# First attention of a pooled-attention and two-MLP kernel: how half of the heads is exponentiated, and where the first weight conversion is asked for

## The chip, the cores and the metric

The kernel runs on one core of one Trainium2 chip. The metric is device microseconds of one execution; of the kernel before three runs are shown, with a median of 1615.76 us (1615.23 to 1616.89). One further execution was profiled, and every row below comes from it.

## The reference

The inputs are `q`, `k`, `v` of shape 8 x 8 x 576 x 64 (batch, heads, positions, head width) in fp32. Keys and values are averaged over groups of 8 positions, which leaves 72 of each.

```python
scores = scale * np.matmul(q, k_p.transpose(0, 1, 3, 2))
scores = scores - np.max(scores, axis=-1, keepdims=True)
attn = np.exp(scores)
attn = attn / (np.sum(attn, axis=-1, keepdims=True) + 1e-09)
out = np.matmul(attn, v_p)
```

The result, 4608 tokens of width 512, goes through two MLPs (512 to 2048 to 512): the first with `h / (1 + exp(-h))`, the second with `h * clip(h + 3, 0, 6) / 6`. The MLP weights are fp64 and are turned into fp32 by the kernel itself from their two 32-bit words; that is the weight conversion spoken of below.

## The kernel before

The 4608 tokens are cut into 36 tiles of 128 rows, and four tiles make a group of 512 tokens, the unit of the MLPs. Matrix products are made of fp32 numbers split into a high and a low part.

Everything stands inside `with tc.manual_schedule()` (L686): the order in which the program asks for instructions is the order in which each engine has them, and no planner rearranges it. Loads go through the queue of SP.

**The first attention** (L709 to L774) makes the first four tiles, 0 to 3, before the first MLP's loop begins. Per tile:

- `scores` (L343) puts q times the pooled keys into two PSUM banks, one for each half of the heads (4 heads of 72 scores, 288 columns).
- `soft` (L742) turns scores into exponentials. For the first half, `below_max` (L366) takes the maxima on VectorE (L369) and subtracts them (L370), and `exps` (L376) is one exponential on ScalarE over 288 columns (L377). For the second half, `max_exps` (L379) takes the maxima on VectorE (L383), multiplies them by minus the scale (L384), and asks ScalarE for four exponentials of 72 columns with the maxima as bias, each of which also gives the sum of its row (L386).
- `turn` (L748) makes `norm` (L397) on VectorE: the sums of the first half (L401), two small instructions on the sums (L402, L405), and the product of all 576 columns with the inverse sums (L406). Then `probs_T` (L408) transposes the probabilities on TensorE (L417), behind some warming matmuls (L341), and ScalarE copies the result out (L418). For tile 3 the norm is asked for by itself (L764), ahead of its `turn`.
- `attend` (L753) is the product with the pooled values on TensorE (L457), and `split_x` splits it into a high part (ScalarE, L473) and a low part (VectorE, L474).

The order is soft 0, soft 1, turn 0, soft 2, turn 1, soft 3, attend 0, turn 2, norm 3, conversion, split 0, attend 1, turn 3, split 1, and so on. Tiles 0 and 1 share one buffer for the copied transposes, so the copies of tile 1 wait for attend 0.

**The weight conversion** is `conv_a` (L727), which takes the next piece from a list and calls `split_a` (L101). For the first piece that is a copy with a scale on ScalarE (L110), then a shift (L113), a shift-and-or (L116) and an and-or (L126) on VectorE, each of which needs the one before it. It issues no DMA and nothing on GpSimd. `conv_b` (L733) later makes the high part on ScalarE (L150) and the low part on GpSimd (L151). Four more pieces are converted at L775 to L778, and further ones in the loop.

**The loop** (L793) is over groups and over 16 slices of the hidden width: 12 matmuls of the first weight (L492), the activation (L506, L507), and the products with the second weight (L536 in the first group). Within the first group it also converts the remaining weights and makes the next attention tiles; their scores (L353) need the pooled keys of the second batch (L290 on VectorE).

Of the kernel before, what the change touches and what calls it, by code (L numbers as in the profile page):

```python
# [10 lines left out]
F32 = mybir.dt.float32  # L11
F32R = mybir.dt.float32r
U32 = mybir.dt.uint32
AF = mybir.ActivationFunctionType
ALU = mybir.AluOpType
AX = mybir.AxisListType
# [9 lines left out]
def kernel(  # L26
# [14 lines left out]
    nc = tc.nc  # L41
    B, NPAIR, P, S = k.shape
    H = 2 * NPAIR
# [13 lines left out]
    ESCALE = 1.0 / (POOL * math.sqrt(D))  # L57
# [5 lines left out]
    att = early.enter_context(tc.tile_pool(name="att", bufs=2))  # L63
# [37 lines left out]
    def split_a(layer, f, piece, mul=False):  # L101


        raw = w_raw.pop((layer, f, piece))
        hw = raw[:, :, 1]

        dst = raw[:, :, 1] if piece else None
        mag = att.tile([P, DM], F32, tag="wmag", name="wmag", bufs=4)
        bits = mag.bitcast(U32)
        nc.scalar.activation(mag, hw.bitcast(F32), AF.Copy, scale=2.0 ** -112)  # L110
        if mul:
            nc.scalar.activation(hw.bitcast(F32), hw.bitcast(F32), AF.Sign)
        nc.vector.tensor_scalar(  # L113
            out=bits, in0=bits, scalar1=3, scalar2=None, op0=ALU.logical_shift_left
        )
        nc.vector.scalar_tensor_tensor(  # L116
            out=bits, in0=raw[:, :, 0], scalar=29, in1=bits,
            op0=ALU.logical_shift_right, op1=ALU.bitwise_or,
        )
        if mul:  # L120
            nc.gpsimd.tensor_tensor(
                out=mag if dst is None else dst.bitcast(F32), in0=mag, in1=hw.bitcast(F32),
                op=ALU.mult,
            )
        else:
            nc.vector.scalar_tensor_tensor(  # L126
                out=bits if dst is None else dst, in0=hw, scalar=0x80000000, in1=bits,
                op0=ALU.bitwise_and, op1=ALU.bitwise_or,
            )
        if piece:  # L130
            w_whole[f] = dst.bitcast(F32)
        else:
            w_mag[layer, f, piece] = mag
# [179 lines left out]
    s_t = {}  # L313
    p_t = {}
# [47 lines left out]
    def new_pr(t, tag=None):  # L362
        pr = staging(tag, H * SP) if tag else prs[t % 2][:, :H * SP]
        p_t[t] = pr.rearrange("p (a h s) -> p a h s", a=2, s=SP)

    def below_max(t, a):  # L366
        sc = s_t[t][a]
        mx = att.tile([P, NPAIR, 1], F32, tag="mx", name="mx")
        nc.vector.tensor_reduce(out=mx, in_=sc, op=ALU.max, axis=AX.X)  # L369
        nc.vector.tensor_tensor(  # L370
            out=p_t[t][:, a], in0=sc, in1=mx.to_broadcast([P, NPAIR, SP]), op=ALU.subtract
        )
        if a == 1:
            s_t.pop(t)

    def exps(t, a):  # L376
        nc.scalar.activation(p_t[t][:, a], p_t[t][:, a], AF.Exp, scale=ESCALE)  # L377

    def max_exps(t, a):  # L379

        sc = s_t[t][a]
        mx = att.tile([P, NPAIR, 1], F32, tag="mx", name="mx")
        nc.vector.tensor_reduce(out=mx, in_=sc, op=ALU.max, axis=AX.X)  # L383
        nc.vector.tensor_scalar(out=mx, in0=mx, scalar1=-ESCALE, scalar2=None, op0=ALU.mult)  # L384
        for h in range(NPAIR):
            nc.scalar.activation(  # L386
                p_t[t][:, a, h], sc[:, h], AF.Exp, scale=ESCALE, bias=mx[:, h],
                accum_out=den_of(t)[:, a * NPAIR + h],
            )
        s_t.pop(t)  # L390

    def den_of(t):
        if t not in den_t:
            den_t[t] = att.tile([P, H, 1], F32, tag="den", name="den")
        return den_t[t]

    def norm(t, summed=0):  # L397
        pr = p_t[t].rearrange("p a h s -> p (a h) s")
        den = den_of(t)
        n = H - summed * NPAIR  # L400
        nc.vector.tensor_reduce(out=den[:, :n], in_=pr[:, :n], op=ALU.add, axis=AX.X)  # L401
        nc.vector.tensor_scalar(  # L402
            out=den, in0=den, scalar1=1e-9, scalar2=float(POOL), op0=ALU.add, op1=ALU.mult
        )
        nc.vector.reciprocal(out=den, in_=den)  # L405
        nc.vector.tensor_tensor(out=pr, in0=pr, in1=den.to_broadcast([P, H, SP]), op=ALU.mult)  # L406

    def probs_T(t, tags=A, tag=None, warm=0):  # L408
        pr = p_t.pop(t)
        pT = staging(tag, H * P)[:SP] if tag else att.tile([SP, H * P], F32, tag="pT", name="pT", bufs=1)  # L410
        pT = pT.rearrange("p (h t) -> p h t", t=P)
        for a in range(2):
            ps = bank(tags, a)
            if a == 0:
                keep_warm(ps, warm)
            for i in range(NPAIR):
                nc.tensor.transpose(ps[:SP, i * P:(i + 1) * P], pr[:, a, i, :], ident)  # L417
            nc.scalar.activation(  # L418
                pT[:, a * NPAIR:(a + 1) * NPAIR, :],
                ps[:SP].rearrange("p (h t) -> p h t", t=P),  # L420
                AF.Copy,
            )
        pT_t[t] = lambda h, o, n: pT[:, h, o:o + n]
# [26 lines left out]
    def weighted(t, tags=A):  # L450
        pT = pT_t.pop(t)
        ps = bank(tags, 0)
        for j in range(NPAIR):
            for o, n, b, _ in halves(t):
                for e in range(2):
                    h = 2 * j + e
                    nc.tensor.matmul(  # L457
                        ps[e * D:(e + 1) * D, j * P + o:j * P + o + n],
                        vp[b % 2][:, h * D:(h + 1) * D],
                        pT(h, o, n),  # L460
                        start=True,
                        stop=True,
                    )
        return ps

    def split_x(t, ps):
        g, i = divmod(t, TPG)
        if i == 0:
            new_x(g)
        xh, xl = xs[g]  # L470
        pv = ps.rearrange("p (j t) -> p j t", t=P)
        sl = slice(i * P, (i + 1) * P)
        nc.scalar.activation(xh[:, :, sl], pv, AF.Copy)  # L473
        nc.vector.tensor_tensor(  # L474
            out=xl[:, :, sl], in0=pv, in1=xh[:, :, sl].bitcast(F32), op=ALU.subtract
        )
# [209 lines left out]
    with tc.manual_schedule():  # L686
# [40 lines left out]
        def conv_a(n, mul):  # L727
            for i in range(n):
                if conv:
                    done.append(conv.pop(0))  # L730
                    split_a(*done[-1], mul=(i < mul))
# [10 lines left out]
        def soft(t):  # L742
            new_pr(t, f"o{4 + t}")
            below_max(t, 0)
            exps(t, 0)
            max_exps(t, 1)

        def turn(t):  # L748
            if t < 3:
                norm(t, 1)  # L750
            probs_T(t, banks[t], f"i{2 + t}" if t > 1 else None, WARM[t + 1] if t < 3 else 0)

        def attend(t):  # L753
            return weighted(t, [banks[t][0]])

        soft(0)
        soft(1)
        turn(0)
        soft(2)
        turn(1)  # L760
        soft(3)
        pv0 = attend(0)
        turn(2)
        norm(3, 1)  # L764
        conv_a(1, 0)
        split_x(0, pv0)
        pv1 = attend(1)
        turn(3)
# [23 lines left out]
        for layer in range(1):  # L792
            for g in range(NG):  # L793
# [4 lines left out]
                for f in range(NF):  # L798
                    n = (layer * NG + g) * NF + f
# [57 lines left out]
                    if 1 in now:  # L857
                        norm(t1)
# [163 lines left out]
```

## Time and profile before

| what | us |
|---|---|
| median of three runs | 1615.76 |
| the profiled execution's own time | 1616.97 |
| its span, first to last instruction | 1615.2 |
| PE busy | 1591.8 (99%) |
| DVE busy | 982.8 (61%) |
| ACT busy | 628.9 (39%) |
| POOL busy | 367.9 (23%) |

PE is TensorE, PEld its weight loads, DVE VectorE, ACT ScalarE, POOL GpSimd. The busy share is an average over the whole span; the stage of the change lies in the first 33 us. Times in rows count from the first instruction.

### The profile page before, as it was taken

How to read it: one execution, taken by the hardware profiler on the slowest of the kernel's cores; microseconds unless marked ns; L12 is line 12 of the kernel's file. 1: busy time of each engine (PE TensorE's matmuls, PEld its weight loads, DVE VectorE, ACT ScalarE, POOL GpSimd, SP SyncE). 2: the span in 40 equal slices, each digit the busy share in tenths (PEclk: the TensorE clock that was granted, in tenths of full speed). 3: DMA queues.
4: the chain of work that ended last, by engine and by line, in shares of the span. 5: the costliest groups of instructions: out<-in, count | busy, mean ns of one | idle time of the engine just before them, and what ended most of it. 6: DMA issues, size and time to landing. Idle time of an engine off the chain costs nothing.

```text
span 1615.2 us, 24007 instructions
## 1 busy us (share of the span) xinstructions
PE 1591.8 (99%) x9214; PEld 1386.5 (86%) x9214; DVE 982.8 (61%) x1592; ACT 628.9 (39%) x1094; POOL 367.9 (23%) x377
## 2 busy tenths in 40 slices
PE   7899999999999999999999999999999999999999
PEld 6455788888888888888888999999999999999998
DVE  7986666676776666665532555555646555656464
ACT  5343564333333333333332334343434343334333
POOL 4643353122312231311011021212121202020200
PEclk9999999999999999999999999999999999999999
DMA  9451245244443544343156634343434353534341
GB/s 282 148 193 41 97 153 163 91 162 149 142 137 121 162 155 131 122 141 126 68 195 208 223 106 159 114 157 105 157 105 157 105 164 98 170 98 163 105 131 53
DMA packets 101331, 224.27 MB, mean 139 GB/s; under 512 B 10464, under 2 KB 35936, under 8 KB 101216
## 3 DMA queue, kind: packets, MB, share of 16 engines
q1 hardware_dynamic: 101216, 222.73, 42.5%
q8 instruction: 73, 1.20, 0.3%
q14 instruction: 42, 0.34, 0.1%
HBM read 169.74 MB, written 52.95 MB: 138 GB/s over the span
## 4 chain that ended last, share of the span: by engine, by line
PE 92%; DVE 3%; DMA 3%; ACT 1%; issue 0%; SPq 0%
PE y L556 44%; PE hps L492 22%; PE p L631 17%; PE y L536 4%; PE aps L457 2%; PE aps L353 2%; ACT gh L654 1%; DVE gl L655 1%; DMA stage<-in_v_dram 1%; DVE t L647 1%; DMA stage<-in_q_dram 1%; DMA wraw<-in_moe_w_out_dram 1%; DVE u L903 0%; DMA wraw<-in_moe_w_in_dram 0%; DVE c L903 0%
## 5 line engine op out<-in xcount | busy, mean ns | idle before, releaser
L492 PE MATMUL hps<-x,whl 128*128 128x512 f32 x1728 | 403.4, 383 | 4.2 <-POOL whl L151 2.1
L492 PEld LDWEIGHTS hps<-x,whl 128*128 128x128 f32 x1728 | 326.1, 189 | 58.9 <-issue 8.0
L631 PEld LDWEIGHTS p<-xst,wst 128*128 128x128 f32 x3024 | 359.6, 192 | 7.6
L631 PE MATMUL p<-xst,wst 128*128 128x256 f32 x3024 | 360.3, 275 | 0.0
L556 PE MATMUL y<-whl,gh 128*128 128x512 f32 x1152 | 343.1, 379 | 0.2 <-ACT gh L654 0.2
L556 PE MATMUL y<-gh,whl 128*128 128x512 f32 x1024 | 310.0, 384 | 0.0
L556 PEld LDWEIGHTS y<-whl,gh 128*128 128x128 f32 x1152 | 207.3, 190 | 23.5 <-ACT gh L654 0.4
L619 POOL TENSOR_TENSOR xst<-xr,xst 128x512 fp32r<-128x512 f32 x63 | 83.4, 1325 | 614.4 <-ACT xst L618 574.7
L556 PE MATMUL y<-whl,gl 128*128 128x512 f32 x576 | 219.2, 381 | 0.6
L556 PEld LDWEIGHTS y<-gh,whl 128*128 128x128 f32 x1024 | 189.4, 189 | 29.4 <-issue 2.9
L556 PE MATMUL y<-gl,whl 128*128 128x512 f32 x512 | 194.6, 380 | 0.0
L655 DVE TENSOR_TENSOR gl<-t,gh 128x512 fp32r<-128x512 f32 x144 | 113.7, 790 | 131.1 <-ACT gh L654 131.1
L512 DVE SCALAR_TENSOR_TENSOR hps<-t,hps 128x512 f32<-128x512 f32 x128 | 88.2, 689 | 170.3 <-ACT t L511 169.7
L511 ACT ACTIVATE t<-hps 128x512 f32<-128x512 f32 x128 | 76.4, 597 | 263.8 <-PE hps L492 262.0
L654 ACT ACTIVATE gh<-t 128x512 fp32r<-128x512 f32 x144 | 119.6, 831 | 151.3 <-DVE t L647 151.3
L903 DVE TENSOR_TENSOR u<-u,p 128x512 f32<-128x512 f32 x180 | 120.1, 684 | 66.2 <-PE p L631 62.0
L193 POOL TENSOR_TENSOR hs<-hmag,hs 128x256 fp32r<-128x256 f32 x88 | 64.2, 734 | 411.2 <-ACT hs L192 367.3
L647 DVE SCALAR_TENSOR_TENSOR t<-t,u 128x512 f32<-128x512 f32 x108 | 90.8, 841 | 89.5 <-ACT t L646 89.5
L521 DVE TENSOR_TENSOR gl<-hps,gh 128x512 fp32r<-128x512 f32 x128 | 88.5, 691 | 85.1 <-ACT gh L520 85.1
L646 ACT ACTIVATE t<-u,three 128x512 f32<-128x512 f32 x108 | 77.4, 717 | 161.0 <-DVE u L903 161.0
L556 PEld LDWEIGHTS y<-whl,gl 128*128 128x128 f32 x576 | 108.8, 189 | 19.4 <-DVE gl L655 4.2
L520 ACT ACTIVATE gh<-hps 128x512 fp32r<-128x512 f32 x128 | 76.6, 598 | 123.8 <-DVE hps L512 123.8
(91 smaller groups left out, 1449.8 us busy)
## 6 DMA issues: line engine op xcount, KB each, us to landing
wst<-ws SPq DMA_DIRECT2D x156, 512.0 KB
ws<-hs SPq DMA_DIRECT2D x56, 256.0 KB
bl<-bT SPq DMA_DIRECT2D x28, 384.0 KB
x<-o SPq DMA_DIRECT2D x36, 256.0 KB
xr<-x SPq DMA_DIRECT2D x36, 256.0 KB
out_dram<-o SPq DMA_DIRECT2D x36, 256.0 KB
wraw<-in_moe_w_in_dram SPq DMA_DIRECT2D x16, 512.0 KB
wraw<-in_moe_w_out_dram SPq DMA_DIRECT2D x16, 512.0 KB
```

The costliest lines, as they stand in the source:

```text
L492: nc.tensor.matmul(ps, w[:, c, :], shuffled(x[:, c, :]), start=(c == 0 and n == 0), stop=(c == NKC - 1 and n == 2),)
L512: nc.vector.scalar_tensor_tensor(out=ps, in0=t, scalar=1.0, in1=ps, op0=ALU.add, op1=ALU.mult)
L520: nc.scalar.activation(in_two(gh), dealt(ps), AF.Copy)
L521: nc.vector.tensor_tensor(out=in_two(gl), in0=dealt(ps), in1=in_two(gh).bitcast(F32), op=ALU.subtract)
L556: nc.tensor.matmul(ps, a, shuffled(b), start=(f == FIRST[layer] and n == 0), stop=(f == LAST[layer] and n == 2),)
L619: nc.gpsimd.tensor_tensor(out=t[:, 1], in0=src, in1=t[:, 0].bitcast(F32), op=ALU.subtract)
L631: nc.tensor.matmul(ps[:, j * HW:(j + 1) * HW], w[:, j, a, c, :], shuffled(x[:, b, c, :]), start=(j == 0 and n == 0 and c == 0), stop=(j == ...
L646: nc.scalar.activation(t, h, AF.Relu, bias=three)
L647: nc.vector.scalar_tensor_tensor(out=t, in0=t, scalar=6.0, in1=h, op0=ALU.min, op1=ALU.mult)
L654: nc.scalar.activation(oh, t3, AF.Copy)
L655: nc.vector.tensor_tensor(out=ol, in0=t3, in1=oh.bitcast(F32), op=ALU.subtract)
L903: nc.vector.tensor_tensor(out=out, in0=a, in1=b, op=ALU.add)
```

## The change

For the second half of the heads `max_exps` goes: `soft` calls `below_max` and `exps` for it as for the first half, so VectorE subtracts the maxima and ScalarE makes one exponential of 288 columns without sums. `norm` sums all 8 heads on VectorE. And the first `conv_a(1, 0)`, which stood behind `norm(3)`, stands behind `soft(3)`, ahead of `attend(0)` and of `turn(2)`, which holds the norm of tile 2.

```diff
-    def max_exps(t, a):
-
-        sc = s_t[t][a]
-        mx = att.tile([P, NPAIR, 1], F32, tag="mx", name="mx")
-        nc.vector.tensor_reduce(out=mx, in_=sc, op=ALU.max, axis=AX.X)
-        nc.vector.tensor_scalar(out=mx, in0=mx, scalar1=-ESCALE, scalar2=None, op0=ALU.mult)
-        for h in range(NPAIR):
-            nc.scalar.activation(
-                p_t[t][:, a, h], sc[:, h], AF.Exp, scale=ESCALE, bias=mx[:, h],
-                accum_out=den_of(t)[:, a * NPAIR + h],
-            )
-        s_t.pop(t)
-
-    def norm(t, summed=0):
+    def norm(t):
         pr = p_t[t].rearrange("p a h s -> p (a h) s")
         den = den_of(t)
-        n = H - summed * NPAIR
-        nc.vector.tensor_reduce(out=den[:, :n], in_=pr[:, :n], op=ALU.add, axis=AX.X)
+        nc.vector.tensor_reduce(out=den, in_=pr, op=ALU.add, axis=AX.X)
...
             new_pr(t, f"o{4 + t}")
             below_max(t, 0)
             exps(t, 0)
-            max_exps(t, 1)
+            below_max(t, 1)
+            exps(t, 1)
 
         def turn(t):
             if t < 3:
-                norm(t, 1)
+                norm(t)
             probs_T(t, banks[t], f"i{2 + t}" if t > 1 else None, WARM[t + 1] if t < 3 else 0)
...
         soft(3)
+        conv_a(1, 0)
         pv0 = attend(0)
         turn(2)
-        norm(3, 1)
-        conv_a(1, 0)
+        norm(3)
         split_x(0, pv0)
```

## Rows read from the trace of the kernel before

**Rows 1.** Busy time by stretch: length, engines, granted PE clock (1.00 is full), DMA share.

```profile
33.20:65.00 31.80, 20.77 (x76) 12.08 (x75) 30.51 (x33) 17.36 (x26) 19.84 (x16) 0.95 0.53 180
65.00:1615.00 1550.00, 1545.40 (x8962) 1352.44 (x8962) 929.74 (x1515) 595.76 (x1016) 332.07 (x332) 1.00 0.42 135
```

**Rows 2.** Timeline of PE: start, duration, instruction, idle time before and its releaser.

```profile
18.90 2.26 PE L341 MATMUL aps<-ident 128*128 128x128 f32 x10
20.99 1.04 PE L417 MATMUL aps<-ident,stage 128*72 128x128 f32 x8
21.86 0.83 PE L341 MATMUL aps<-ident 128*128 128x128 f32 x6
22.53 1.04 PE L417 MATMUL aps<-ident,stage 128*72 128x128 f32 x8
23.50 1.09 PE L457 MATMUL aps<-pT,vp 72*64 72x128 f32 x16
24.52 0.94 PE L341 MATMUL aps<-ident 128*128 128x128 f32 x6
25.62 1.04 PE L417 MATMUL aps<-ident,stage 128*72 128x128 f32 x8 [0.16 <-DVE stage L406]
...
28.69 1.04 PE L417 MATMUL aps<-ident,stage 128*72 128x128 f32 x8 [1.01 <-DVE stage L406]
...
65.03 0.74 PE L353 MATMUL aps<-kbd,qT 128*64 128x144 f32 x2 [5.40 <-DVE kbd L290]
```

**Rows 3.** Timeline of ACT, 24 to 29 us.

```profile
24.70 1.08 ACT L418 ACTIVATE pT<-aps 72x512 f32<-72x512 f32 x2 [0.47 <-PE aps L457]
25.67 0.44 ACT L377 ACTIVATE stage<-stage 128x288 f32<-128x288 f32 x1
26.01 0.31 ACT L386 ACTIVATE stage<-aps,mx 128x72 f32<-128x72 f32 x1
...
28.15 0.68 ACT L110 ACTIVATE wmag<-wraw 128x512 f32<-128x512 f32 x1
```

**Rows 4.** Timeline of DVE, 19 to 34 us, and one sum of the loop.

```profile
19.36 1.52 DVE L406 TENSOR_TENSOR stage<-stage,den 128x576 f32<-128x576 f32 x1
...
21.28 0.46 DVE L370 TENSOR_TENSOR stage<-aps,mx 128x288 f32<-128x288 f32 x1
...
23.07 0.45 DVE L401 TENSOR_REDUCE den<-stage 128x4 f32<-128x288 f32 x1 [0.57 <-ACT stage L377]
...
27.34 0.17 DVE L402 TENSOR_SCALAR den<-den 128x8 f32<-128x8 f32 x1 [0.75 <-ACT stage L386]
...
27.79 0.76 DVE L406 TENSOR_TENSOR stage<-stage,den 128x576 f32<-128x576 f32 x1
28.86 0.43 DVE L113 TENSOR_SCALAR wmag<-wmag 128x512 uint32<-128x512 uint32 x1 [0.31 <-ACT wmag L110]
...
30.05 0.70 DVE L126 SCALAR_TENSOR_TENSOR wmag<-wraw,wmag 128x512 uint32<-128x512 uint32 x1
30.67 2.61 DVE L474 TENSOR_TENSOR x<-aps,x 128x512 fp32r<-128x512 f32 x4
33.19 0.42 DVE L113 TENSOR_SCALAR wmag<-wmag 128x512 uint32<-128x512 uint32 x1
...
73.43 0.75 DVE L401 TENSOR_REDUCE den<-pr 128x8 f32<-128x576 f32 x1 [0.51 <-ACT pr L377]
```

**Rows 5.** Busy time by stretch, columns as in Rows 1: around two waits of PE.

```profile
18.90:20.90 2.00, 2.00 (x11) 2.00 (x11) 1.91 (x4) 0.00 (x0) 1.92 (x3) 0.50 1.05 418
65.00:68.60 3.60, 3.56 (x6) 1.62 (x7) 3.52 (x5) 0.00 (x0) 2.30 (x2) 0.50 0.81 254
68.60:72.00 3.40, 3.40 (x10) 1.62 (x9) 3.33 (x5) 0.00 (x0) 3.24 (x4) 0.98 0.10 42
```

**Rows 6.** DVE by line and shape, 33 to 66 us: busy, mean ns of one.

```profile
L116 DVE SCALAR_TENSOR_TENSOR wmag<-wraw,wmag 128x512 uint32<-128x512 uint32 x10 | 12.1, 1208 | 0.3
L113 DVE TENSOR_SCALAR wmag<-wmag 128x512 uint32<-128x512 uint32 x10 | 8.4, 838 | 0.8 <-ACT wmag L110 0.7
```

## The prediction

> **What bounds the kernel now.** The busy time by stretch comes first. From 65 us to the end PE is busy 1545.40 of 1550.00 us [rows 1]: whatever makes the point at 65 us later or earlier makes the end so too, unless PE finds work to save, and the change touches none of PE's work there. Before that, from 33.2 to 65 us, DVE is busy 30.51 of 31.80 us and PE only 20.77 [rows 1]; PE's last long wait in it, 5.40 us, ends at 65.03 on VectorE's pooled keys [rows 2]. So from 33.19, where the second weight conversion starts on VectorE [rows 4], VectorE's queue is the path. It can start that conversion only after the last low part of x (the L474 group that begins at 30.67 [rows 4]), and that needs attend 3, which stands behind the transposes of tile 3 on PE. The timeline of PE shows what they wait for: 28.69, after 1.01 us of idleness that VectorE's norm of tile 3 ends [rows 2]. The number that matters is therefore when these transposes start. All that follows them is one chain: copies, attends 2 and 3, split of x, next conversion.
>
> **Part 1, the exponentials.** Per tile ScalarE loses four exponentials and their sums, which run from 26.01 to about 27.3, where L402 that waited for them begins [rows 3, 4], and gains one that lasts 0.44 [rows 3]. VectorE gains 0.46 (subtraction, L370) for the small L384, for which I take the 0.17 of the nearest row, L402, and 0.75 for 0.45 in the sum [rows 4]: 0.29 and 0.30, so 0.59 us a tile.
> For tiles 0 and 1 this is covered. By the end of norm 1 VectorE has three subtractions and two sums more, 3 x 0.29 + 2 x 0.30 = 1.47 us. Norm 1 ended at 19.36 + 1.52 = 20.88, so it ends at 22.35 at worst, and from a norm's end to the transposes it takes 0.14 (27.79 + 0.76 = 28.55 to 28.69): 22.49. PE, busy without a gap from 18.90 on, comes to the transposes of tile 1 at 22.53 [rows 2, 4]. If VectorE's waits grew, the cover would be gone by the excess, some tenths.
> For tile 3, had nothing else been moved, the second exponential would end at 26.01 + 0.44 = 26.45, the sum at about 27.23, and L402 would start at 27.27 instead of 27.34: a gain of 0.1 us. That is all that this part is worth; ScalarE's saved time lies beside waits on PE (0.47 us ahead of the copies at 24.70 [rows 3]).
>
> **Part 2, the moved conversion.** Its instructions are L110 on ScalarE and L113, L116, L126 on VectorE; no DMA, nothing for GpSimd, and no queue of DMAs is passed. On VectorE it now stands behind soft 3 and ahead of norm 2 and norm 3. L113 needs L110, and L110 stands on ScalarE behind the exponentials of tile 3, these behind the copies of tile 1, and these wait for attend 0 on PE, which ends where the warming matmuls begin, 24.52; nothing in the change makes that earlier. So the new wait holds norm 2, whose inputs are there long before, and behind it norm 3 and the low parts of x; for norm 2 wait the transposes of tile 2, and in PE's queue behind them attend 1, the transposes of tile 3, attends 2 and 3 and the first MLP.
> The times, step by step:
> - First exponential of tile 3 at 25.67, as before; the second 0.34 later at 26.01 [rows 3]; L110 another 0.34 later at 26.35; with its 0.68 it ends at 27.03. If its weights had landed only just before 28.15 it would start then, 1.8 later; I take nothing for this, since that load is the first of its kind in the queue, and keep 1.8 for the far end.
> - L113 starts 0.03 after L110's end (28.83 to 28.86), at 27.06. From L113 to the instruction behind L126 it is 30.67 - 28.86 = 1.81 [rows 4]: norm 2 starts at 28.87. Before, its sum began at 23.07 [rows 4].
> - One norm is the sum, 0.75 and 0.04 to the next, and then 27.34 to 28.55, 1.21: 2.00 us [rows 4]. Norm 2 ends at 30.87, norm 3 at 32.87.
> - Transposes of tile 2: 30.87 + 0.14 = 31.01, against 25.62. They take 0.97 (22.53 to 23.50) and attend 1 takes 1.02 (23.50 to 24.52) [rows 2]: PE reaches tile 3 at 33.00, and norm 3 allows 32.87 + 0.14 = 33.01. Against 28.69 that is 4.32 us late.
> - PE's clock. PE has nothing between the end of its warming matmuls, 24.52 + 0.94 = 25.46, and 31.01: 5.55 us. After the 5.40 us of idleness that end at 65.03 the granted clock is 0.50 (1.2 instead of 2.4 GHz) until 68.60 and then back at 0.98 [rows 2, 5]. So I put the work of 31.01 to about 34.6 at the lower level. Warming matmuls at 0.50 take (20.99 - 18.90) / 10 = 0.209 us, at full clock (22.53 - 21.86) / 6 = 0.112, a factor of 1.87 [rows 2, 5]. On 0.97 + 1.02 = 1.99 us that adds 1.73. Bounds: nothing, if the clock holds, and 0.87 x (1.99 + 0.97 + 2 x 1.02) = 4.35, if it stays low to the end of attend 3.
> Sum: 4.32 + 1.73 = 6.05 us for the transposes of tile 3. The conversion has left its place behind norm 3, 1.81 us of VectorE, but this is no gain: the split of x now waits for attend 3, and the second conversion for the split, as far behind tile 3's transposes as before.
> Does the rest pass it on? VectorE's work from 33.19 on is the same and hangs together with ScalarE's and GpSimd's copies and products of the same pieces, so it moves as a whole: 6.05 at 65 us, and from there PE carries it. SP's loads that wait for attends move with them.
>
> **A rule.** In rows 3 the first exponential of tile 3, whose subtraction ended at 21.74 [rows 4], lets ScalarE stand idle for 0.47 us ahead of the copies at 24.70 and starts only behind them: ScalarE keeps its order. No row shows a ready instruction held on VectorE; I take it to do the same. The Trainium skill, "PSUM — Partial Sum Buffer", section "Engine vs sequencer instructions", says that the queues of ScalarE, VectorE and GpSimd are strictly first in, first out; by it norm 2 is held, and the 6.05 us stand. It speaks against this change: without it the sum would be the 0.1 us gain of part 1.
>
> **Against which time.** The rows' execution took 1616.97 us, 1.77 around its span of 1615.2 included, and would take 1623.0. It lies 1.21 above the median, 1615.76; I forecast against the median: 1615.76 + 6.05 = 1621.8.
>
> **The rivals.**
> - The clock holds. For it: what PE did before the two waits differs, warming matmuls and transposes here, wide matmuls there; against it: the idle time is as long, 5.55 against 5.40 us, and after the latter the clock was low [rows 2, 5]. Time: 4.32, 1620.1.
> - The clock stays low through attend 3: 4.32 + 4.35 = 8.7, 1624.4. Against it: at 68.60 it was back after 3.6 us of work.
> - VectorE does not hold norm 2, or the conversion's copy runs early enough. To cost nothing, norm 3 must end by 28.55; with 2.00 for each norm and 1.81 ahead of them L113 must start by 22.74, while ScalarE has the copies and exponentials of rows 3 still before it. Time: 1615.7.
> - Not slower, by a lighter meeting of VectorE and GpSimd. From 33 to 66 us L116 takes 1208 ns on average and L113 838 [rows 6], but 0.70 (the like L126) and 0.43 in the first conversion [rows 4], where GpSimd is idle. Ten of each: 5.1 + 4.1 = 9.2 us that VectorE loses there. If the new order let the two engines miss each other, up to 9.2 would come back, and 1615.76 + 6.05 - 9.2 = 1612.6 is the end; it decides from 6.05 us on, two thirds of all meetings. Against it: the meetings are set by the hand-over of one piece from engine to engine, and that is unchanged.
>
> **How the numbers follow.** About 0.2%, 3.2 us, is what a measurement of this kernel can tell from no change. Forecast 0.55; the clock holds 0.17; the clock stays low 0.09; no hold, or most of it given back later, 0.14; more than all of it given back 0.05. The first three are slower by more than 0.2%: 0.81; the fourth is the same, 0.14; the fifth faster, 0.05. The range takes in the two cases of the clock and some giving back below the smaller: 1617.5 to 1625.0. The 1.8 us for late weights would reach 1623.6.
>
> **What would show it.** Right: on VectorE a wait of some 4 us for L110 ends near 27.06, and norm 2 comes behind L126 near 28.87; the transposes of tile 2 start near 31.0 after 5.5 us of PE idleness, at a clock of 0.50; those of tile 3 start near 34.7; the second conversion's L113 at 39.2 instead of 33.19; pooled keys release PE near 71. Wrong: norm 2 ahead of L113 on VectorE, L110 ahead of tile 3's exponentials, a full clock at 31 us, or PE's wait at 65 us ending less late than tile 3's transposes did.

## The result, and the profile after

The changed kernel takes 1624.33 us (median of 4 runs, 1624.13 to 1627.09) against 1616.33 us of the kernel before in the same series: a ratio of 1.0053, 95% interval 1.0035 to 1.0070. It is 8.0 us slower; forecast were 6.05.

The profiled execution of after is the slowest of the four (1627.09 us). Of its 10.1 us more span, 1.89 us are there before the change can act on PE: its transposes of tile 1 begin at 24.42 instead of 22.53, behind a later load of q and a clock that stayed low for longer. A second profile of the same kernel (below) begins at 21.36. Times from here on are therefore also counted from attend 0, which the change does not move.

The timeline of PE, after; columns as in [rows 2].

```profile
22.15 1.76 PE L403 MATMUL aps<-ident,stage 128*72 128x128 f32 x8
23.75 0.83 PE L341 MATMUL aps<-ident 128*128 128x128 f32 x6
24.42 1.04 PE L403 MATMUL aps<-ident,stage 128*72 128x128 f32 x8
25.39 1.09 PE L443 MATMUL aps<-pT,vp 72*64 72x128 f32 x16
26.41 0.94 PE L341 MATMUL aps<-ident 128*128 128x128 f32 x6
32.84 1.89 PE L403 MATMUL aps<-ident,stage 128*72 128x128 f32 x8 [5.49 <-DVE stage L392]
34.66 1.98 PE L443 MATMUL aps<-pT,vp 72*64 72x128 f32 x16
36.56 1.92 PE L403 MATMUL aps<-ident,stage 128*72 128x128 f32 x8
38.42 3.68 PE L443 MATMUL aps<-stage,vp 72*64 72x128 f32 x32
...
74.89 0.50 PE L353 MATMUL aps<-kbd,qT 128*64 128x144 f32 x1 [5.44 <-DVE kbd L290]
```

L403 are the transposes, L443 the attends. The transposes of tile 2 waited 0.16 us for VectorE before [rows 2]; now it is 5.49 us. And the transposes and attends from 32.84 on take nearly twice their time: 1.89 for 1.04, 3.68 for two attends of 1.09 each. Why VectorE is late shows in its timeline, with ScalarE's behind it; columns as in [rows 3, 4].

```profile
21.36 0.46 DVE L370 TENSOR_TENSOR stage<-aps,mx 128x288 f32<-128x288 f32 x1
28.91 0.43 DVE L113 TENSOR_SCALAR wmag<-wmag 128x512 uint32<-128x512 uint32 x1 [7.10 <-ACT wmag L110]
29.38 0.69 DVE L116 SCALAR_TENSOR_TENSOR wmag<-wraw,wmag 128x512 uint32<-128x512 uint32 x1
30.10 0.69 DVE L126 SCALAR_TENSOR_TENSOR wmag<-wraw,wmag 128x512 uint32<-128x512 uint32 x1
30.71 0.74 DVE L387 TENSOR_REDUCE den<-stage 128x8 f32<-128x576 f32 x1
...
32.61 0.74 DVE L387 TENSOR_REDUCE den<-stage 128x8 f32<-128x576 f32 x1
...
43.38 0.42 DVE L113 TENSOR_SCALAR wmag<-wmag 128x512 uint32<-128x512 uint32 x1
```

```profile
24.45 0.76 ACT L377 ACTIVATE stage<-stage 128x288 f32<-128x288 f32 x2
26.59 1.08 ACT L404 ACTIVATE pT<-aps 72x512 f32<-72x512 f32 x2 [1.39 <-PE aps L443]
27.56 0.77 ACT L377 ACTIVATE stage<-stage 128x288 f32<-128x288 f32 x2
28.23 0.65 ACT L110 ACTIVATE wmag<-wraw 128x512 f32<-128x512 f32 x1
```

The exponentials of tile 2 end at 25.21 (24.45 + 0.76). The sum of norm 2 (L387) could run then and starts at 30.71, because L113 stands ahead of it and waits for L110, and L110 stands on ScalarE behind the copies of tile 1 and the exponentials of tile 3. VectorE is idle for 7.10 us, and for the last 3.70 of them (25.21 to 28.91) the sum is ready.

Busy time by stretch, after; columns as in [rows 1].

```profile
30.50:47.00 16.50, 13.47 (x74) 10.81 (x75) 9.77 (x17) 8.32 (x15) 2.92 (x3) 0.50 0.67 197
65.00:1625.00 1560.00, 1550.11 (x8990) 1355.71 (x8988) 939.01 (x1526) 599.63 (x1022) 339.06 (x339) 1.00 0.42 135
```

The granted clock is 0.50 (1.2 GHz) from 30.5 to 47 us although PE is busy 13.47 of these 16.50 us. From the second conversion (43.38) to the keys (74.89) it is 31.51 us, against 33.19 to 65.03, 31.84, before [rows 2, 4]; and from 65 us on PE is busy 1550.11 of 1560.00 us, so it carries what is late to the end.

### The profile page after: what moved, and what is told of

Read it like the earlier page. It is cut to its first block, busy times and chain, and to the rows that moved or that the text cites. A ratio compares the mean times of both kernels' runs of the same rounds, so it can differ in the third digit from the quotient of the medians.

```text
span 1625.3 us, 23970 instructions
## 1 busy us (share of the span) xinstructions
PE 1599.0 (98%) x9214; PEld 1392.2 (86%) x9214; DVE 982.8 (60%) x1592; ACT 625.3 (38%) x1066; POOL 367.5 (23%) x377
## 4 chain that ended last, share of the span: by engine, by line
PE 92%; DVE 4%; DMA 2%; ACT 1%; issue 1%; SPq 0%; DVEq 0%
PE y L542 44%; PE hps L478 22%; PE p L617 18%; PE y L522 4%; PE aps L443 2%; PE aps L353 2%; DMA wraw<-in_moe_w_in_dram 1%; DMA stage<-in_k_dram 1%; ACT gh L640 1%; DVE gl L641 1%; DVE t L633 1%; DVE u L890 0%; PE aps L403 0%; DVE wmag L116 0%; DVE c L890 0%
```

## The experiments

For each kernel: the median and the ratio to the kernel before in the same series, and in its one profile the time from attend 0 to PE's release by the second batch's keys. Before that is 23.50 to 65.03, 41.53 us [rows 2]; after, 25.39 to 74.89, 49.50.

| kernel | median us | ratio, 95% interval | attend 0 to keys, us |
|---|---|---|---|
| exponentials alone | 1616.13 | 0.9997, 0.9987 to 1.0006 | 41.48 |
| move alone | 1624.39 | 1.0049, 1.0036 to 1.0062 | 50.08 |
| change, warming kept up | 1620.67 | 1.0024, 1.0014 to 1.0034 | 45.89 |
| conversion between norms 2 and 3 | 1620.27 | 1.0020, 1.0011 to 1.0029 | 44.80 |
| exponentials of tile 3 earlier | 1616.17 | 0.9998, 0.9989 to 1.0007 | 40.67 |
| the same, conversion ahead of norm 2 | 1622.42 | 1.0036, 1.0023 to 1.0049 | 47.69 |
| keys on GpSimd, ahead | 1614.26 | 0.9985, 0.9976 to 0.9994 | no wait |
| the change again | 1624.53 | 1.0050, 1.0035 to 1.0065 | 47.56 |
| keys on GpSimd, in the loop | 1617.26 | 1.0003, 0.9994 to 1.0012 | 42.44 |
| keys in the loop, exponentials earlier | 1616.88 | 1.0000, 0.9990 to 1.0009 | 42.06 |
| keys shared | 1612.66 | 0.9971, 0.9960 to 0.9982 | no wait |
| keys shared, exponentials earlier | 1611.77 | 0.9971, 0.9959 to 0.9982 | no wait |

**Which part of the change.** The exponentials alone:

```diff
         soft(3)
-        conv_a(1, 0)
         pv0 = attend(0)
         turn(2)
         norm(3)
+        conv_a(1, 0)
```

> The exponentials as in the changed kernel, the conversion where it was before. Theory A (the time is lost because VectorE's wait for the conversion's copy holds norm 2): as before, 1616.3 within 1.5 us, transposes of tile 3 near 28.6 us when those of tile 1 start at 22.5. Theory B (VectorE's added work, 0.59 us a tile, is the loss): near 1624.

Measured 1616.13, and 41.48 us against 41.53. In this profile tile 1's transposes began earlier, at 20.11, and those of tile 3 follow 6.09 us later (26.20), where theory A has 6.1. The move alone, in the kernel before:

```diff
         soft(3)
+        conv_a(1, 0)
         pv0 = attend(0)
         turn(2)
         norm(3, 1)
-        conv_a(1, 0)
```

> The old exponentials with their sums, the conversion asked for ahead of norm 2. Theory A: slower like the change, 1623 to 1626; the four exponentials end 0.9 us later than the one, so L113's wait ends 0.9 us later, and the two shorter sums give 0.6 back. Theory B: as before, 1616.3.

Measured 1624.39. Within the intervals the move is the whole loss; theory B falls with both. PE's timeline of the move alone shows the wait even longer, since the old four exponentials keep L110 back for longer: L113 starts 4.38 us after attend 0 (25.58 and 21.20), against 3.52 in the change (28.91 and 25.39). The last line, attends 2 and 3, again takes nearly twice its time.

```profile
29.20 1.90 PE L417 MATMUL aps<-ident,stage 128*72 128x128 f32 x8 [6.05 <-DVE stage L406]
...
34.78 3.68 PE L457 MATMUL aps<-stage,vp 72*64 72x128 f32 x32
```

**Hold and clock apart.** The change with PE kept at work by more warming matmuls (each counts as two in the profile: 3 are the x6 of [rows 2], 26 the x52 below):

```diff
-WARM = (0, 5, 3, 3)
+WARM = (0, 5, 3, 26)
```

> The changed kernel with 26 instead of 3 warming matmuls ahead of the transposes of tile 2, about 5.8 us of them at full clock, so that PE does not idle while norm 2 is held. Theory A with the clock as its second term: norm 2 still starts near 28.9 us, the granted clock stays 1.00, the transposes of tile 3 come 4.3 us late instead of 6 to 8: 1620.6. If the clock costs nothing and the hold is all: 1624.3, as the change.

Measured 1620.67. VectorE still waits, but PE's granted clock no longer falls in this wait. Timelines of PE and VectorE, and one stretch:

```profile
22.83 6.07 PE L341 MATMUL aps<-ident 128*128 128x128 f32 x52
29.26 1.04 PE L403 MATMUL aps<-ident,stage 128*72 128x128 f32 x8 [0.36 <-DVE stage L392]
...
31.26 1.07 PE L403 MATMUL aps<-ident,stage 128*72 128x128 f32 x8
```

```profile
25.34 0.43 DVE L113 TENSOR_SCALAR wmag<-wmag 128x512 uint32<-128x512 uint32 x1 [2.94 <-ACT wmag L110]
```

```profile
29.20:34.20 5.00, 4.94 (x64) 4.19 (x64) 3.08 (x6) 3.84 (x8) 0.11 (x1) 1.00 0.83 192
```

The clock is 1.00, a group of transposes takes 1.04 again, and from attend 0 (21.81) to those of tile 3 it is 9.45 us against 28.69 - 23.50 = 5.19 before [rows 2]: 4.26 us of hold alone, where 4.32 were worked out. The clock's part is the rest: 1624.33 - 1620.67 = 3.7 us between the medians. This figure is rough, since the single runs of either kernel spread over some 4 us; in the last column of the table it is 49.50 - 45.89 = 3.61 us with the change's first profile and 47.56 - 45.89 = 1.67 with its second.

**Moving the hold.** Norm 2 ahead of the conversion, norm 3 behind it:

```diff
         def turn(t):
-            if t < 3:
+            if t < 2:
                 norm(t)
...
         soft(3)
+        norm(2)
         conv_a(1, 0)
```

> The changed kernel with norm 2 ahead of the conversion on VectorE and norm 3 behind it; ScalarE's copy still right behind the exponentials of tile 3. Theory A: transposes of tile 2 as before (3.1 us behind those of tile 1), norm 3 starts near 28.9 us, transposes of tile 3 near 31.0 against 28.7: 2.3 us slower at full clock, up to 4.9 if PE's 3.4 us of idleness lower it, so 1618.6 to 1621.2. Theory B: as the change, 1624.

Measured 1620.27. The wait goes from tile 2 to tile 3, as expected: tile 3's transposes come 7.47 us after attend 0 (29.11 and 21.64), 2.28 later than before, where 2.3 were forecast. They still run at full clock (1.04); the granted clock falls to 0.50 at about 30.4, and the attends behind them take 3.46:

```profile
24.29 1.04 PE L403 MATMUL aps<-ident,stage 128*72 128x128 f32 x8 [0.69 <-ACT stage L377]
25.25 1.09 PE L443 MATMUL aps<-pT,vp 72*64 72x128 f32 x16
29.11 1.04 PE L403 MATMUL aps<-ident,stage 128*72 128x128 f32 x8 [2.76 <-DVE stage L392]
30.07 3.46 PE L443 MATMUL aps<-stage,vp 72*64 72x128 f32 x32
```

The time of the eleven runs of this one kernel goes with the granted clock: the five whose mean is 0.996 or more took 1617.66 to 1619.03 us, the six at 0.995 or less 1620.27 to 1621.44.

**Moving what the hold waits for.** First the exponentials of tile 3 ahead of the copies of tile 1, with the conversion behind norm 3:

```diff
         soft(2)
-        turn(1)
+        norm(1)
         soft(3)
+        turn(1, True)
```

Here `turn(1, True)` leaves the norm out, since `norm(1)` has asked for it.

> The changed kernel's exponentials, the conversion back behind norm 3, and the exponentials of tile 3 on ScalarE ahead of the copies of tile 1 (VectorE's order unchanged). Theory A: norm 3 no longer waits for ScalarE, and the transposes of tile 3 come 0.4 to 1.1 us earlier after those of tile 1 than with the exponentials alone: 1615.0 to 1615.9 us. If ScalarE's order is not what norm 3 waits for: 1616.1, as with the exponentials alone.

Measured 1616.17, which can't be told from 1616.1; the profile has 40.67 us, 0.86 less than before, and tile 3's transposes follow attend 1 without a wait. Expected was up to 1615.9: not shown by the times. Then the same order with the conversion ahead of norm 2:

```diff
         soft(3)
+        conv_a(1, 0)
         turn(1, True)
```

> The changed kernel's order on VectorE, with the conversion ahead of norm 2, but on ScalarE the exponentials of tile 3 and the conversion's copy ahead of the copies of tile 1. Theory A: L113's wait ends about 2.4 us earlier, and so do norm 2 and 3: transposes of tile 3 some 1.9 us later than before at full clock, 1618.3 us, up to 1620.8 if PE's 3.1 us of idleness lower it. Rival (the place on VectorE costs the time, however early the copy is): 1624.3, as the change.

Measured 1622.42, above the 1620.8 that I allowed, and 2.1 us below the change in the same series (1624.53); of the runs of the two only one of either lies within the other's spread. L113 now starts 1.67 us after attend 0 (23.80 and 22.13) instead of 3.52 (28.91 and 25.39). The hold is shorter by this; but PE still idles for 3.64 us, and its clock is low from there to the end of attend 3:

```profile
27.70:37.00 9.30, 9.27 (x64) 7.45 (x64) 3.76 (x7) 4.46 (x8) 1.28 (x1) 0.50 0.64 160
```

I had allowed for the low clock for less long. With the 4.35 us that the prediction gives for a low clock through attend 3 the sum is 1618.3 + 4.35 = 1622.65. The rival, that the place on VectorE costs the same however early the copy is, misses by 1.9 us.

**The change again.**

> The changed kernel once more, for a second profile. Theory A: VectorE's wait for L110 and PE's wait of 5.5 us stand in it as in the first, and from attend 0 to PE's release by the second batch's keys it is 49.5 us again, 8 us more than before; the 1.9 us by which tile 1's transposes began later in the first profile belong to that execution and are not there in every one.

Measured 1624.53, but the profile has 47.56 us and not 49.50. PE's timeline and the stretches around:

```profile
22.32 1.09 PE L443 MATMUL aps<-pT,vp 72*64 72x128 f32 x16
...
29.77 1.89 PE L403 MATMUL aps<-ident,stage 128*72 128x128 f32 x8 [5.49 <-DVE stage L392]
31.60 1.90 PE L443 MATMUL aps<-pT,vp 72*64 72x128 f32 x16
33.43 1.07 PE L403 MATMUL aps<-ident,stage 128*72 128x128 f32 x8
34.43 1.97 PE L443 MATMUL aps<-stage,vp 72*64 72x128 f32 x32
...
69.88 0.74 PE L353 MATMUL aps<-kbd,qT 128*64 128x144 f32 x2 [5.44 <-DVE kbd L290]
```

```profile
29.70:33.40 3.70, 3.62 (x24) 2.87 (x24) 2.32 (x5) 1.67 (x3) 0.00 (x0) 0.51 0.78 212
33.40:38.00 4.60, 3.80 (x46) 3.26 (x45) 2.10 (x5) 3.87 (x8) 1.27 (x1) 1.00 0.49 132
```

The wait is the same, 5.49 us; here the clock came back at 33.4, ahead of tile 3. This execution is the forecast's: 47.56 - 41.53 = 6.03 us. The first profile is the rival with the clock low through attend 3: 7.97.

**Is VectorE's queue the path, and what would help?** The second batch's keys off VectorE, in the kernel with the exponentials alone, asked for on GpSimd behind soft 3 and not in the loop:

```diff
         soft(3)
+        for j in range(NPAIR):
+            pool_k(1, j, nc.gpsimd)
...
-                    if n < 3:
-                        for j in ((0, 1), (2,), (3,))[n]:
-                            pool_k(1, j)
```

> The exponentials as in the changed kernel, the conversion behind norm 3, and the pooled keys of the second batch made on GpSimd behind soft 3 instead of by eight sums of 0.75 us on VectorE inside its full stretch from 33 to 65 us. If VectorE's queue there is the path and PE carries what it ends with (theory A): 4 to 6 us faster, 1610 to 1612. If another wait stands right behind it: 1616.1.

Measured 1614.26: faster, but by 2.4 us and not 4 to 6. GpSimd's timeline tells why, with PE's first MLP matmuls:

```profile
27.80 1.17 POOL L280 TENSOR_TENSOR stage<-stage 128x288 f32<-128x288 f32 x1 [6.33 <-DMA stage<-in_k_dram]
...
37.58 1.26 POOL L151 TENSOR_TENSOR whl<-wmag,whl 128x512 fp32r<-128x512 f32 x1
```

```profile
38.90 7.38 PE L478 MATMUL hps<-x,whl 128*128 128x512 f32 x20 [7.44 <-POOL whl L151]
```

It is the change's own fault on another queue. The keys wait 6.33 us for their load and then take 9.8 us (27.80 to 37.58). The first low part, L151, stands behind them and starts at 37.58, though the high part that it needs from ScalarE (L150) ends at 29.31, and PE waits 7.44 us for it. Next, the keys on GpSimd at their places in the loop:

```diff
-                            pool_k(1, j)
+                            pool_k(1, j, nc.gpsimd)
```

> The exponentials alone, and the second batch's pooled keys on GpSimd at their old places in the loop, where GpSimd was idle for 5.6 us behind the second conversion, instead of ahead of the first conversion, where they waited for their load and held GpSimd's low part. Theory A (VectorE's queue from 33 to 65 us is the path, and a front instruction that waits holds all behind it): no wait of 7 us on GpSimd, eight sums of 0.75 us off VectorE: 3 to 6 us faster than before, 1610 to 1613.5. If GpSimd's added work meets VectorE's as often as it relieves it: 1615 to 1616.5.

Measured 1617.26, not to be told from the 1616.95 of before in this series, so theory A missed: GpSimd is the path now, and PE waits for its last key:

```profile
66.02 0.74 PE L353 MATMUL aps<-kbd,qT 128*64 128x144 f32 x2 [7.77 <-POOL kbd L285]
```

The same with the exponentials of tile 3 earlier:

> The same with the exponentials of tile 3 ahead of the copies of tile 1 on ScalarE. Theory A: 0 to 1 us less than with the keys alone.

Measured 1616.88; 0.4 us less can't be told from none. Last, only the two keys that fit GpSimd's idle time, and the last key one slice earlier:

```diff
-                    if n < 3:
-                        for j in ((0, 1), (2,), (3,))[n]:
-                            pool_k(1, j)
+                    if n < 2:
+                        for j in ((0, 1), (2, 3))[n]:
+                            pool_k(1, j, None if n else nc.gpsimd)
```

> The exponentials alone; of the second batch's four keys the first two are pooled on GpSimd in the loop's first slice, where GpSimd was idle for 5.6 us, and the last two on VectorE in the second slice, one slice earlier for the last. Theory A: no wait of PE for the keys (5.4 us before, 7.8 with all four on GpSimd), 3 us less on VectorE, and PE carries the gain: 3 to 5 us faster than before, ratio 0.997 to 0.998. If conversions stand right behind the keys: ratio 1.000.

Measured 1612.66, 0.29% faster than before. PE no longer waits for the keys, its clock does not fall there, and the next wait is 3.74 us. The profile puts it down to L110, but it ends 0.15 us after VectorE's norm of that tile (L392, 70.89 + 0.76 = 71.65), whose product the transposes read; VectorE was at weight conversions until 67.4 and came to the tile only then:

```profile
55.41 1.20 PE L353 MATMUL aps<-kbd,qT 128*64 128x144 f32 x16
56.54 4.59 PE L522 MATMUL y<-t,wraw 128*128 128x512 f32 x8
60.47 3.27 PE L478 MATMUL hps<-x,whl 128*128 128x512 f32 x12
63.57 4.49 PE L522 MATMUL y<-t,wraw 128*128 128x512 f32 x8
71.80 1.67 PE L403 MATMUL aps<-ident,pr 128*72 128x128 f32 x8 [3.74 <-ACT wmag L110]
```

> The same with the exponentials of tile 3 ahead of the copies of tile 1 on ScalarE. Theory A: 0 to 1 us less.

Measured 1611.77, the lowest median of all, but with the same ratio as without the earlier exponentials, so that their gain is not shown. Both beat the kernel before and the changed one.

## Why the prediction was right, and where a size was off

- **The path.** Right: what tile 3's transposes lose, the keys and the end lose. Between the second conversion and the keys 0.33 us were given back in the first profile and none in the second (37.90 to 69.88, 31.98 us against 31.84).
- **Part 1.** Right: 0.1 us was forecast, and the exponentials alone can't be told from before. Its cover was read off one execution, though. In the profile of the exponentials alone PE's clock stays full through the first attention, tile 1's transposes could begin earlier, and they wait 1.35 us for norm 1; with the old exponentials, in the move alone, they wait 1.72. So this wait isn't the change's either.
- **The hold.** Right in every step. Less the 1.89 us of the later start, norm 2 starts at 28.82 (28.87 forecast), tile 2's transposes at 30.95 (31.01) and tile 3's at 34.67 (34.7). VectorE's wait was put at some 4 us and is 7.10 in the first profile, 3.93 in the second; only its end counts. With the warming kept up the hold alone is 4.26 us in the profile (4.32 forecast) and 4.3 us between the medians (1620.67 and 1616.38).
- **VectorE keeps its order.** No row of before showed it; now one does: the sum of norm 2, ready at 25.21, starts behind L126 at 30.71. The Trainium skill, "PSUM — Partial Sum Buffer", section "Engine vs sequencer instructions", has said so of ScalarE, VectorE and GpSimd, and the traces agree for VectorE (5.50 us between ready and start) and, with the keys ahead, for GpSimd (L151, ready at 29.31, starts at 37.58).
- **The clock.** The mis-sized term. I took 1.73 us, with the low clock to end about when tile 3's transposes begin, as in [rows 5], and gave 0.09 to its lasting through attend 3 (4.35 us). The medians put it at some 3.7 us. In the first profile the second conversion, 41.49 after the same subtraction, is 2.3 us behind the 39.2 forecast, all of it between tile 3's transposes and attend 3; in the second profile the clock is back in time and the sum of the forecast holds. In three of the four profiles with a wait at tile 2 (the change's first, the move alone, and the conversion ahead with earlier exponentials) the clock was low through attend 3; so the case to which I gave the smaller chance was the more frequent one, as far as four profiles tell. What was wrong was to take the 3.6 us of [rows 5] for the length of the low stretch: from PE's restart it was 3.6 us in one of these profiles and 13.5 to 14.7 us in the other three. Why, is open.
- **Lighter meetings of VectorE and GpSimd.** Did not come: 0.33 us at most, in place of 9.2.

## What to carry to other kernels

An engine that keeps its order pays for an instruction by when its inputs come, not by how long it runs: 1.8 us of work, asked for ahead of a step that was ready, cost 4.3 us on VectorE, and the same mistake on GpSimd, with keys whose load was late, made PE wait 7.4 us. So ask for work behind what is ready sooner, and put it where the engine's idle time begins after its inputs have come. A wait that leaves TensorE idle can have a second price in its clock, here some 3.7 us beside the 4.3 of the hold; put it into the sum with both ends.

## What was not expected of the hardware

How long the clock stays low after PE is at work again varies from one execution to the next for the same instructions: after 5.49 us of idleness it came back 3.6 us after the restart in the second profile of the change (29.77 to 33.4), and only at about 47.5, 14.7 us after the restart, in the first, there after the wide matmuls of the first MLP had run for 4.7 us (from 42.80). In the second profile it fell once more, at about 43.6, during a wait of 2.05 us; in the kernel before it stayed at 1.00 over a wait of 2.06 at the same place (37.77 to 39.83). What decides is left open; no run tells it apart.

With all keys on GpSimd in the loop, a VectorE instruction on 8 columns took 2.09 us, for 0.17 in [rows 4], and 2.09 again in the run with the earlier exponentials. Timelines of VectorE and of GpSimd, that kernel:

```profile
69.05 2.09 DVE L388 TENSOR_SCALAR den<-den 128x8 f32<-128x8 f32 x1
```

```profile
68.60 1.28 POOL L121 TENSOR_TENSOR wraw<-wmag,wraw 128x512 f32<-128x512 f32 x1
69.84 1.26 POOL L151 TENSOR_TENSOR whl<-wmag,whl 128x512 fp32r<-128x512 f32 x1
```

It ends at 71.14, just behind the second of two GpSimd instructions that follow each other (71.10). The Trainium skill, "SBUF — State Buffer", section "Who interferes with whom", says that the two engines share a pair of ports under an exclusive lock, that `tensor_scalar` is among the VectorE operations that can take the pair under certain conditions, and that the loser blocks until the other's instruction is over. The times agree, and if the lock is the cause, the loser here missed its turn a second time; no run tests that cause.
